# First loads in halves, fewer warm-up products and a reordered head in a gated dilated convolution

## The chip, the cores and the metric

The kernel runs on one core of a Trainium2 chip. The core has TensorE (PE) for matrix products, with its weight loads shown apart (PEld), VectorE (DVE), ScalarE (ACT), GpSimd (POOL) and SyncE (SP), which here only issues DMAs. Products go to PSUM, eight banks; everything else lies in SBUF. The metric is the time of one execution on the device in microseconds, the median of several runs; less is better.

## The reference

A causal convolution with three taps two tokens apart, a gate, and a projection. B = 2, T = 16000, D = 256, all in bfloat16:

```python
pad = 4
xp = jnp.pad(x, ((0, 0), (pad, 0), (0, 0)))
h = sum over i of 0, 1, 2:  xp[:, pad - 2*i : pad - 2*i + T, :] @ w[i]   # w: 3 x 256 x 512
z = jnp.tanh(h[..., :256]) * sigmoid(h[..., 256:])
return z @ w_o                                                           # w_o: 256 x 256
```

So a token needs itself, the token two back and the one four back. The notation of the sum is shortened; the reference adds the three products one after another.

## The kernel before, in words

Channels lie on partitions (256 channels are two halves, `ct` 0 and 1), tokens run along the free dimension, sorted by phase: token `4 r + j` or `8 r + j` is column `r` of phase `j`. Most of the work goes in "wide" groups of rows of eight tokens, whose tokens come by transposing DMAs (`load_wide`, L128). For them the three taps are not multiplied one by one: sums and differences of token phases (`wide_pairs` L221, `wide_p` L228, `wide_m` L232, `wide_d` L241, on DVE and in part on POOL) are multiplied by sums and differences of the taps' weights, in a scheme that needs fewer products than the three taps taken directly. The results are unscrambled by ACT (`keep_first` L286, `keep_second` L290), POOL (`other` L293) and DVE (`split_bank` L296, `rest` L300). Then ACT applies tanh and sigmoid (L340, L344), DVE multiplies the two (L349), PE projects (L374), and the result is copied out of PSUM and stored by SP.

A block is one group with 128 (plain) or, in the two narrow wide groups, 256 of the 512 output channels. `blocks` 0 to 3 are the plain group of the first 512 tokens, 4 and 5 the first wide group `G0`, 6 and 7 the second, `G1`, both 128 rows wide; later wide groups have 256 rows and four blocks each. Three small extra groups are multiplied directly beside them.

The schedule is written out by hand: every engine runs its instructions in the order in which the program issues them, and semaphores follow from the data and the buffers. The order of the head, which the change touches:

1. Loads (L141 to L145). SP: the first 512 tokens as 128 rows of four tokens (`xn`), then the taps `w_taps[TAPS[1]]`, that is tap 0. ACT: `TAPS[0]` (tap 2) and `TAPS[2]` (tap 1), then the table of functions. SP goes on with the transposing loads, one after another.
2. Seven warm-up products of 512 columns on constants (L149).
3. `turn` (L176 to L184) four times: for each half `h` of the phases and each half `ct` of the channels two PE transposes into a PSUM tile, and a copy to the plain group's tile `groups[0]["x"]`. For `h` 0 the PSUM tile is from the pool `ps_o` (two buffers), for `h` 1 from `ps_y` (three). The copies are ACT's for `ct` 0 and DVE's for `ct` 1.
4. The first tap of the four plain blocks (`direct`, L316): block 0 in two halves of the phases, blocks 1 to 3 whole. Then `weight_mm` (L170), six products that build combined weights in PSUM, then the second tap (tap 0) of the four blocks, and further on the third.
5. The combined weights: on DVE `plus2`/`minus2` (L440), `ws` (L444), `wmh` (L445) and `make_wu` (L455); on POOL `wph` (L446); on ACT `wd0`, `wm`, `wd2` (L447 to L449) and `make_wt` (L452). `make_wt` and `make_wu` of one `ct` read the same PSUM tile.
6. DVE's sums of `G0` and `G1`, and the first products of blocks 4 and 5 (`first`, L259).

From block 4 on a loop over the blocks (L553 to L632) issues for each: `second` and `keep_second`, `rest` of the block before, `third`, `split_bank`, the steps that the dictionaries `small`, `big` and `mid` hold for this block, and `late` in two parts. `late(V, 0)` adds to the two PSUM banks that `rest(V)` reads, and `late(V, 1)` adds to the same banks afterwards, so it waits for `rest(V)`. The list `mid[ND]` holds what DVE does behind block 4's `split_bank`.

Of the kernel before, what the change touches and what calls it, by code (L numbers as in the profile page):

```python
# [13 lines left out]
def kernel(  # L14
# [23 lines left out]
    nc = tc.nc  # L38
    bf16 = mybir.dt.bfloat16
    f32 = mybir.dt.float32  # L40
    B, T, D = x.shape
    K, _, D2 = w.shape
    P = 128
    assert K == 3 and D % P == 0 and D2 == 2 * D and T % 64 == 0
    CT = D // P
# [6 lines left out]
    TAPS = (2, 0, 1)  # L52
# [4 lines left out]
    for b in range(B):  # L57
        t, stop = (4 * 2 * P if b == 0 else 0), (T - 4 * RE if b == B - 1 else T)
        while t < stop:
            n = min(need, (stop - t) // 8)  # L60
# [23 lines left out]
    ps_y = ctx.enter_context(tc.tile_pool(name="ps_y", bufs=3, space=bass.MemoryType.PSUM))  # L84
    ps_o = ctx.enter_context(tc.tile_pool(name="ps_o", bufs=2, space=bass.MemoryType.PSUM))
    ctx.enter_context(tc.manual_schedule())

    def new_y():
        return ps_y.tile([P, 2, BANK], f32, name="y")
# [47 lines left out]
    w_taps = [consts.tile([P, CT, D2], bf16, name=f"w{k}_sb") for k in range(K)]  # L137
    wo_sb = consts.tile([P, NT, D], bf16)
    xn = osb_pool.tile([P, 4, D], bf16, name="osb")
    w_in = [w[k].rearrange("(ct c) d -> c ct d", c=P) for k in range(K)]  # L140
    nc.sync.dma_start(out=xn[:], in_=x[0, 0:4 * P, :].rearrange("(r j) c -> r j c", j=4))  # L141
    for k in (TAPS[0], TAPS[2]):
        nc.scalar.dma_start(out=w_taps[k][:], in_=w_in[k])
    nc.scalar.preload_act_table(ACT.Sigmoid)
    nc.sync.dma_start(out=w_taps[TAPS[1]][:], in_=w_in[TAPS[1]])  # L145
    for n in range(7):
        if n < 3:
            wps = new_y()
        nc.tensor.matmul(wps[:, 1, :], lhsT=warm[:, :P], rhs=warm, start=n < 3, stop=True, skip_group_check=True)  # L149
# [15 lines left out]
    def weight_mm():  # L165

        for ct in range(CT):
            y = W["y", ct] = ps_o.tile([P, D2], f32, name="wt_ps", tag="o_ps")
            for tap in (2, 0, 1):
                nc.tensor.matmul(  # L170
                    y[:], lhsT=twos[tap != 2][:], rhs=w_taps[tap][:, ct, :],
                    start=tap == 2, stop=tap == 1, skip_group_check=True,
                )


    def turn(h, ct):  # L176
        if h == 0:
            tp = ps_o.tile([P, 2, P], bf16, name="tp", tag="o_ps")[:]
        else:
            tp = ps_y.tile([P, 2, P], bf16, name="tq", tag="y")[:]  # L180
        for j in range(2):
            nc.tensor.transpose(out=tp[:, j, :], in_=xn[:, 2 * h + j, ct * P:(ct + 1) * P], identity=ident[:])  # L182
        copy = nc.vector.tensor_copy if ct % 2 else nc.scalar.copy
        copy(out=groups[0]["x"][:, 2 * h:2 * h + 2, ct, RH:RH + P], in_=tp)  # L184

    def views(G):
        xt, R = G["x"], G["R"]
        return xt[:, 0:2, :, RH - 1:RH - 1 + R], xt[:, 2:4, :, RH - 1:RH - 1 + R]

    def tap1_columns(G, ct):  # L190

        xt, R = G["x"], G["R"]
        lead = xt[:, 2:4, ct, RH - 1:RH - 1 + R]
        dims = [list(p) for p in lead.ap]
        return bass.AP(
            tensor=lead.tensor, offset=lead.offset,
            ap=[dims[0], [1 - 2 * CT * (RH + R), 2], [CT * (RH + R), 2], [1, R]],
        )

    def pair(G, i, back0, back1, col, rows):  # L200

        first = G["x"][:, 2 * i:2 * i + 2, :, col - back0:col - back0 + rows]
        dims = [list(p) for p in first.ap]
        return bass.AP(
            tensor=first.tensor, offset=first.offset,
            ap=[dims[0], [2 * CT * XW + back0 - back1, 2], [XW, 2 * CT], [1, rows]],
        )
# [3 lines left out]
    def sums(G, nm):  # L211
        if nm not in G:
            G[nm] = q_pool.tile(SUMS[nm], bf16, name=nm, bufs=3 if nm == "qd" else 2)
        return G[nm]

    def wide_pairs(G, h):

        for col, sl in G["cols"]:
            n = sl.stop - sl.start
            a, s = pair(G, 0, 0, 0, col, n), pair(G, 2, 0, 1, col, n)  # L220
            ins = nc.vector.tensor_tensor(  # L221
                out=sums(G, "q")[:, h, :, :, :, sl].rearrange("p h q ct r -> p h (q ct) r"),
                in0=s, in1=a, op=ALU.subtract if h else ALU.add)
        return ins

    def wide_p(G):
        q = G["q"][:, 0, :, :, :, :G["R"]]
        return nc.vector.tensor_tensor(out=sums(G, "qp")[..., :G["R"]], in0=q[:, 0], in1=q[:, 1], op=ALU.subtract)  # L228

    def wide_m(G, h):  # L230
        q = G["q"][:, h, :, :, :, :G["R"]]
        return nc.vector.tensor_tensor(out=sums(G, "qm")[:, h, ..., :G["R"]], in0=q[:, 0], in1=q[:, 1], op=ALU.add)  # L232
# [66 lines left out]
    def rest(B):  # L299
        nc.vector.tensor_tensor(out=B.sv[:], in0=B.sv[:], in1=B.y[:], op=ALU.subtract)  # L300

    def direct(B, taps, out, new=True, h0=None):

        xt, R = B.G["x"], B.R
        for tap in taps:
            if B.G is end:
                parts = [(None, xt[:, 4 - 2 * tap:8 - 2 * tap])]
            elif h0 is not None:
                parts = [(h0, views(B.G)[h0])]
            else:  # L310
                lo = RH if tap == 0 else RH - 1
                parts = [(None, xt[:, :, :, lo:lo + R])]
            for h, mv in parts:
                to = out if h is None else out[:, 2 * h * R:2 * (h + 1) * R]
                for ct in range(CT):
                    nc.tensor.matmul(  # L316
                        to, lhsT=w_taps[tap][:, ct, B.osl[0]],
                        rhs=tap1_columns(B.G, ct) if tap == 1 and B.G is not end else mv[:, :, ct, :],
                        start=new and tap == TAPS[0] and ct == 0 and not h, stop=tap == TAPS[-1] and ct == CT - 1,
                        skip_group_check=True,  # L320
                    )
# [96 lines left out]
    blocks = []  # L418
# [5 lines left out]
    ND = 4  # L424
    NB = len(blocks)

    def bank(B, i):
        return B.y[:, i % 2, :]

    for h in range(2):  # L430
        for ct in range(CT):
            turn(h, ct)
    for k in range(ND):
        blocks[k].y = new_y() if k % 2 == 0 else blocks[k - 1].y
    for h in range(2):
        direct(blocks[0], TAPS[:1], bank(blocks[0], 0), h0=h)
    for k in range(1, ND):
        direct(blocks[k], TAPS[:1], bank(blocks[k], k))
    for i, two in enumerate(twos):
        nc.vector.tensor_scalar_mul(two[:], ident[:], -2.0 if i else 2.0)  # L440
    weight_mm()
    for k in range(ND):
        direct(blocks[k], TAPS[1:2], bank(blocks[k], k))
    nc.vector.tensor_tensor(out=ws_sb[:], in0=w_taps[0][:], in1=w_taps[2][:], op=ALU.add)  # L444
    nc.vector.tensor_tensor(out=W["wmh"][:], in0=ws_sb[:], in1=w_taps[1][:], op=ALU.subtract)  # L445
# [5 lines left out]
    def make_wt(ct):  # L451
        return nc.scalar.copy(out=W["wt"][:, ct, :], in_=W["y", ct][:])  # L452

    def make_wu(ct):
        nc.vector.scalar_tensor_tensor(  # L455
            out=W["wu"][:, ct, :], in0=w_taps[1][:, ct, :], scalar=-4.0, in1=W["y", ct][:],
            op0=ALU.mult, op1=ALU.subtract)

    G0, G1 = groups[1:3]
    make_wu(0)  # L460
    make_wt(1)
    make_wu(1)
    make_wt(0)
    wide_pairs(G0, 0)
    wide_p(G0)
    for k in range(ND):
# [7 lines left out]
    wide_d(G0, 1, nc.vector)  # L474
    wide_d(G0, 0, nc.vector)
    wide_pairs(G1, 0)
    wide_p(G1)
    last = wide_m(G1, 0)

    def extra_block(i, taps):  # L480
        E = extras[i]
# [23 lines left out]
    small, big, mid = {}, {}, {}  # L505

    def do(steps, k):
        ins = None
        for step in steps.pop(k, []):
            ins = step() or ins  # L510
        return ins

    def gates_of(G, dts):
        if dts.stop == NT:
            ready.extend(pieces(G))
        return gate(G, dts)
# [4 lines left out]
        if B.oi % 2 == 1:  # L521
            big.setdefault(k + 1, []).append(lambda: gates_of(B.G, dts))

    mid[ND] = [lambda: wide_pairs(G1, 1)]
    mid[ND + 4] = [lambda: gates_of(extra, slice(0, 2))]
    mid[ND + 6] = [lambda: gates_of(end, slice(0, 2))]
    for G in wides[1:]:
# [25 lines left out]
    for k in range(ND, NB):  # L553
        B, V = blocks[k], (blocks[k - 1] if k > ND else None)
# [17 lines left out]
        last = do(small, k) or last  # L572
# [3 lines left out]
        def big_and_quarter(last):  # L576
            last = do(big, k) or last
            if B.G["n"] > 1 and B.oi == 0:
                quarter(B.G, 3, last)
            elif k in (ND + 2, ND + 3) or B.G["n"] > 1 and B.G["n"] + 1 < len(wides):  # L580
                for i in {ND + 2: (), ND + 3: (2,)}.get(k, (B.oi - 1,)):
                    quarter(wides[B.G["n"] + 1], i, last)
            return last

        if not big_late:
            last = big_and_quarter(last)
# [28 lines left out]
        last = do(mid, k) or last  # L615
        if big_late:
            last = big_and_quarter(last)
# [112 lines left out]
```

## Time and profile before

| | |
|---|---|
| median of 3 runs | 262.14 us (261.97 to 263.0) |
| profiled execution | 261.54 us, span 259.8 us |
| busy, share of the span | PE 254.9 us (98%), ACT 246.1 (95%), DVE 226.0 (87%), POOL 115.3 (44%) |
| instructions | PE 1491 products, 1491 weight loads, DVE 270, ACT 378, POOL 128 |
| DMA | 35.17 MB, 135 GB/s in the mean |

The span runs from the first to the last instruction of the program; the execution's time has 1.74 us around it. A line of the timeline reads: start in us, length, engine, line of the kernel, operation, names of output and inputs, shapes, count; in brackets the idle time of the engine before it and what ended it. A "q" behind an engine's name is its instruction queue, which also issues the DMAs. Matmuls overlap one another, so their lengths add up to more than the time that they take.

### The profile page before, as it was taken

What the parts mean: (1) busy time and instruction counts of PE and PEld (TensorE: products, weight loads), DVE (VectorE), ACT (ScalarE), POOL (GpSimd) and SP (SyncE); (2) the same over time, 40 slices, a digit from 0 to 9 for tenths busy, and PEclk for the clock granted to TensorE, in tenths of its full rate; (3) what the DMA queues carried; (4) which work ended last, traced back from release to release, by engine and by line L of the source; (5) the groups of instructions that cost most, each with busy time, mean ns of one, the idle gap of its engine ahead of it and who ended that gap; (6) DMA issues with size and microseconds to landing.
All of it is one profiled execution on the core that took longest, in us unless ns stands there. A gap on an engine that the chain in (4) does not pass through costs nothing.

```text
span 259.8 us, 4299 instructions
## 1 busy us (share of the span) xinstructions
PE 254.9 (98%) x1491; PEld 146.0 (56%) x1491; DVE 226.0 (87%) x270; ACT 246.1 (95%) x378; POOL 115.3 (44%) x128
## 2 busy tenths in 40 slices
PE   8999999999999999999999999999999999999993
PEld 4577765555555555555555555555555555555572
DVE  2889999988988988999988988988988988986673
ACT  5768889999999999999999999999999999999993
POOL 1432435445445445446445445445445445444240
PEclk9999999999999999999999999999999999999999
DMA  7999782471925628283481925728294221221226
GB/s 199 208 196 213 150 203 81 113 207 50 252 81 125 171 85 210 82 178 116 129 208 40 252 83 111 182 87 209 81 153 142 82 81 43 81 83 43 81 101 222
DMA packets 79685, 35.17 MB, mean 135 GB/s; under 512 B 69552, under 2 KB 72368, under 8 KB 79664
## 3 DMA queue, kind: packets, MB, share of 16 engines
q1 hardware_dynamic: 78560, 33.99, 52.1%
q10 hardware_dynamic: 1104, 0.92, 1.4%
q8 instruction: 11, 0.18, 0.3%
q14 instruction: 10, 0.08, 0.1%
HBM read 1.18 MB, written 16.38 MB: 68 GB/s over the span
## 4 chain that ended last, share of the span: by engine, by line
PE 97%; DVE 0%; ACT 0%; issue 0%; DVEq 0%; ACTq 0%
PE y L259 70%; PE o_ps L374 19%; PE y L316 2%; PE e_ps L316 2%; PE y L149 1%; PE y L374 1%; PE f_ps L316 1%; PE wt_ps L170 0%; DVE osb L674 0%; ACT osb L674 0%; PE tp L182 0%; PE tq L182 0%; DVEq L725 0%; ACT osb L672 0%; DVEq L672 0%
## 5 line engine op out<-in xcount | busy, mean ns | idle before, releaser
L293 POOL TENSOR_TENSOR sv<-sv,st 128x512 f32<-128x512 f32 x60 | 76.5, 1275 | 17.4 <-ACT sv L290 7.9
L241 POOL TENSOR_TENSOR qd<-xq 128x256 bf16<-128x256 bf16 (+2 forms) x58 | 33.7, 585 | 111.4 <-DVE zw L349 54.5
L300 DVE TENSOR_TENSOR sv<-sv,y 128x1024 f32<-128x1024 f32 x60 | 72.7, 1212 | 4.0 <-PE y L259 3.8
L259 PE MATMUL y<-qd,wd_sb 128*128 128x512 bf16 (+1 forms) x256 | 61.6, 366 | 0.0
L411 ACT CAST osb<-o_ps 128x512 bf16<-128x512 f32 x114 | 61.1, 591 | 0.0
L374 PE MATMUL o_ps<-wo_sb,zw 128*128 128x256 bf16 x450 | 58.9, 273 | 0.0
L296 DVE SCALAR_TENSOR_TENSOR y<-st,y 128x512 f32<-128x512 f32 x60 | 41.8, 696 | 19.6 <-PE y L259 11.1
L374 PEld LDWEIGHTS <-zw 128*128 128x128 bf16 x480 | 46.9, 98 | 17.4
L259 PE MATMUL y<-qp,wmh_sb 128*128 128x512 bf16 (+1 forms) x128 | 45.0, 366 | 0.0
L259 PEld LDWEIGHTS <-wd_sb 128*128 128x128 bf16 x256 | 25.0, 98 | 27.4 <-issue 0.5
L221 DVE TENSOR_TENSOR q<-xq 128x2048 bf16<-128x2048 bf16 (+3 forms) x34 | 37.9, 1119 | 0.9 <-DMA xq<-in_x_dram 0.8
L290 ACT ACTIVATE sv<-y 128x512 f32<-128x512 f32 x60 | 35.9, 598 | 0.9 <-PE y L259 0.7
L286 ACT ACTIVATE st<-y 128x512 f32<-128x512 f32 x60 | 36.3, 606 | 0.2 <-PE y L259 0.2
L259 PE MATMUL y<-q,wu_sb 128*128 128x512 bf16 (+1 forms) x128 | 35.7, 366 | 0.0
L259 PE MATMUL y<-qm,wph_sb 128*128 128x512 bf16 (+1 forms) x128 | 35.7, 366 | 0.0
L259 PE MATMUL y<-q,wt_sb 128*128 128x512 bf16 (+1 forms) x128 | 35.7, 366 | 0.0
L259 PE MATMUL y<-qm,wm_sb 128*128 128x512 bf16 (+1 forms) x128 | 35.7, 366 | 0.0
L349 DVE TENSOR_TENSOR zw<-thw,sgw 128x2048 bf16<-128x2048 bf16 x28 | 34.1, 1218 | 0.0
L340 ACT ACTIVATE sgw<-sv 128x1024 bf16<-128x1024 f32 x30 | 32.3, 1078 | 0.7 <-DVE sv L300 0.5
L340 ACT ACTIVATE thw<-sv 128x1024 bf16<-128x1024 f32 x30 | 32.3, 1078 | 0.3 <-DVE sv L300 0.3
L340 ACT ACTIVATE sgw<-y 128x1024 bf16<-128x1024 f32 x30 | 31.3, 1044 | 0.0
L340 ACT ACTIVATE thw<-y 128x1024 bf16<-128x1024 f32 x30 | 31.3, 1043 | 0.0
(68 smaller groups left out, 179.9 us busy)
## 6 DMA issues: line engine op xcount, KB each, us to landing
out_dram<-osb SPq DMA_DIRECT2D x54, 256.0 KB, 2.1
out_dram<-osb SPq DMA_DIRECT2D x10, 128.0 KB, 1.9
w_sb<-in_w_dram ACTq DMA_DIRECT2D x2, 256.0 KB, 4.2
out_dram<-osb SPq DMA_DIRECT2D x2, 160.0 KB, 2.0
xq<-in_x_dram SPq DMA_TRANSPOSE x17, 6.7
osb<-in_x_dram SPq DMA_DIRECT2D x1, 256.0 KB, 2.5
w_sb<-in_w_dram SPq DMA_DIRECT2D x1, 256.0 KB, 3.8
out_dram<-osb ACTq DMA_DIRECT2D x2, 128.0 KB, 2.1
```

What stands on the lines that cost most here:

```text
L221: ins = nc.vector.tensor_tensor(out=sums(G, "q")[:, h, :, :, :, sl].rearrange("p h q ct r -> p h (q ct) r"), in0=s, in1=a, op=ALU.subtract ...
L241: ins = after(eng.tensor_tensor(out=sums(G, "qd")[:, h, q, ct, sl], in0=a, in1=s, op=ALU.subtract), behind)
L259: nc.tensor.matmul(B.y[:, bank, i * n:(i + 1) * n], lhsT=wmat[:, ct, osl], rhs=mv[:, :, ct, :B.R], start=new and ct == 0 and i == 0, stop= ...
L286: nc.scalar.mul(B.st[:], B.y[:, 0, :], 4.0)
L290: nc.scalar.mul(B.sv[:, 0], B.y[:, 0, :], 2.0)
L293: after(nc.gpsimd.tensor_tensor(out=B.sv[:, 1], in0=B.sv[:, 0], in1=B.st[:], op=ALU.subtract), behind)
L296: nc.vector.scalar_tensor_tensor(out=B.y[:, 1, :], in0=B.st[:], scalar=-0.5, in1=B.y[:, 0, :], op0=ALU.mult, op1=ALU.add)
L300: nc.vector.tensor_tensor(out=B.sv[:], in0=B.sv[:], in1=B.y[:], op=ALU.subtract)
L340: nc.scalar.activation(out=dst[:, :, ph].rearrange("p b j c -> p j b c"), in_=at[:].rearrange("p j (b c) -> p j b c", b=hi - lo), func=fun ...
L349: return eng.tensor_tensor(out=z, in0=th, in1=sg, op=ALU.mult)
L374: nc.tensor.matmul(o_ps[q] if isinstance(o_ps, list) else o_ps[:, q, :], lhsT=z_columns(G, rb0, jp, q, dt), rhs=wo_sb[:, dt, :], start=(dt ...
L411: copy(out=G["osb"][:, 2 * h:2 * h + 2, :], in_=o_ps)
```

## The change

- The load of the first tokens becomes two loads by phases (`xn[:, 0:2]`, `xn[:, 2:4]`), both on SP, ahead of tap 0. The load of tap 2 becomes two loads by channels, both on ACT, ahead of tap 1.
- Five warm-up products instead of seven.
- `turn` takes all four PSUM tiles from `ps_o`. The copies are DVE's, but for `(h, ct) = (1, 0)`, which is ACT's.
- The first tap goes by quarters, that is phases half `h` and channels half `ct`, each for all four blocks: sixteen products of 256 columns, in the order (0, 0), (1, 0), (0, 1), (1, 1), with `turn(1, 1)` behind the first quarter and the other three `turn`s ahead of it.
- The second tap of blocks 0 and 1 goes ahead of `weight_mm`.
- `make_wu` and `make_wt` go in the order wu 0, wt 0, wu 1, wt 1 instead of wu 0, wt 1, wu 1, wt 0.
- `wide_m(G1, 0)` moves from ahead of the loop to the first place of `mid[ND]`. POOL's `other` of block 4, which was ordered behind it, is ordered behind `wide_p(G1)`.

```diff
-    nc.sync.dma_start(out=xn[:], in_=x[0, 0:4 * P, :].rearrange("(r j) c -> r j c", j=4))
-    for k in (TAPS[0], TAPS[2]):
-        nc.scalar.dma_start(out=w_taps[k][:], in_=w_in[k])
+    for h in range(2):
+        nc.sync.dma_start(
+            out=xn[:, 2 * h:2 * h + 2, :], in_=x[0, 0:4 * P, :].rearrange("(r j) c -> r j c", j=4)[:, 2 * h:2 * h + 2, :])
+    for ct in range(CT):
+        nc.scalar.dma_start(out=w_taps[TAPS[0]][:, ct, :], in_=w_in[TAPS[0]][:, ct, :])
+    nc.scalar.dma_start(out=w_taps[TAPS[2]][:], in_=w_in[TAPS[2]])
...
-    for n in range(7):
+    for n in range(5):
...
     def turn(h, ct):
-        if h == 0:
-            tp = ps_o.tile([P, 2, P], bf16, name="tp", tag="o_ps")[:]
-        else:
-            tp = ps_y.tile([P, 2, P], bf16, name="tq", tag="y")[:]
+        tp = ps_o.tile([P, 2, P], bf16, name="tp", tag="o_ps")[:]
...
-        copy = nc.vector.tensor_copy if ct % 2 else nc.scalar.copy
+        copy = nc.scalar.copy if (h, ct) == (1, 0) else nc.vector.tensor_copy
...
-    def direct(B, taps, out, new=True, h0=None):
+    def direct(B, taps, out, new=True, h0=None, cts=range(CT)):
...
-                for ct in range(CT):
+                for ct in cts:
...
-    for h in range(2):
-        for ct in range(CT):
-            turn(h, ct)
+    def first_tap(h, ct):
+        for k in range(ND):
+            direct(blocks[k], TAPS[:1], bank(blocks[k], k), h0=h, cts=(ct,))
+
+    for ct in range(CT):
+        turn(0, ct)
+    turn(1, 0)
     for k in range(ND):
         blocks[k].y = new_y() if k % 2 == 0 else blocks[k - 1].y
+    first_tap(0, 0)
+    turn(1, 1)
+    first_tap(1, 0)
     for h in range(2):
-        direct(blocks[0], TAPS[:1], bank(blocks[0], 0), h0=h)
-    for k in range(1, ND):
-        direct(blocks[k], TAPS[:1], bank(blocks[k], k))
+        first_tap(h, 1)
     for i, two in enumerate(twos):
         nc.vector.tensor_scalar_mul(two[:], ident[:], -2.0 if i else 2.0)
+    for k in range(2):
+        direct(blocks[k], TAPS[1:2], bank(blocks[k], k))
     weight_mm()
-    for k in range(ND):
+    for k in range(2, ND):
         direct(blocks[k], TAPS[1:2], bank(blocks[k], k))
...
-    make_wu(0)
-    make_wt(1)
-    make_wu(1)
-    make_wt(0)
+    for ct in range(CT):
+        make_wu(ct)
+        make_wt(ct)
...
-    wide_p(G1)
-    last = wide_m(G1, 0)
+    last = wide_p(G1)
...
-    mid[ND] = [lambda: wide_pairs(G1, 1)]
+    mid[ND] = [lambda: wide_m(G1, 0), lambda: wide_pairs(G1, 1)]
```

## The prediction

> **What bounds the kernel now.** I read the page first, then busy time by stretch, then the chain in order of time, then the timeline of the first 23 us by engine. The page and the chain of what ended last:
>
> ```profile
> span 259.8 us, 4299 instructions
> PE 97%; DVE 0%; ACT 0%; issue 0%; DVEq 0%; ACTq 0%
> ```
>
> The chain is TensorE (PE) almost alone. By stretches (busy us and count for PE, PEld, VectorE = DVE, ScalarE = ACT, GpSimd = POOL; granted clock; DMA share; GB/s):
>
> ```profile
> 13.50:22.70 9.20, 9.20 (x70) 6.66 (x69) 8.77 (x12) 6.77 (x12) 3.55 (x3) 1.00 1.29 210
> 45.00:240.00 195.00, 195.00 (x1103) 107.73 (x1101) 176.74 (x202) 195.00 (x301) 94.03 (x105) 1.00 0.48 126
> ```
>
> PE has no hole in either, so from 0.77 us on every microsecond taken out of PE's queue ends the kernel earlier, unless another engine then ends last. DVE is the candidate: 8.77 of 9.20 us in the stretch behind the head, against 177 of 195 later. The change touches only the head, so the head's chain comes next (start, length, what):
>
> ```profile
> 0.77 3.15 PE y L149 x7
> 3.92 0.43 PE tp L182 x4
> 4.77 1.97 PE y L316 x10
> 6.74 1.29 PE wt_ps L170 x6
> 8.04 3.47 PE y L316 x16
> ```
>
> and the same products by form in the head (count, busy us, mean ns of one):
>
> ```profile
> L149 PE MATMUL y<-const-bfloat16-1.0 128*128 128x512 bf16 x7 | 3.1, 625 | 0.8 <-PEq L714 0.8
> L316 PE MATMUL y<-xt,w_sb 128*128 128x512 bf16 x22 | 5.1, 380 | 0.0
> L182 PE MATMUL tp<-ident,osb 128*128 128x128 bf16 x4 | 0.6, 311 | 0.0
> ```
>
> The same 512 columns take 625 ns from start to end in the warm-up and 380 behind it, so PE runs at about half rate at first. Sixteen products at full rate took 3.47, 0.217 each; four transposes at low rate 0.43, 0.107 each. The change of rate lies between the transposes and L316's first products, near 4.7 us.
>
> **The change part by part.** What the head waits for now:
>
> ```profile
> 0.73 1.00 ACTq L143 DMA_DIRECT2D w_sb<-in_w_dram  x2
> 0.74 0.40 SPq L141 DMA_DIRECT2D osb<-in_x_dram  x1
> 1.20 0.41 SPq L145 DMA_DIRECT2D w_sb<-in_w_dram  x1
> 1.65 4.70 SPq L128 DMA_TRANSPOSE xq<-in_x_dram  x1
> 2.44 0.15 PEld L149 LDWEIGHTS <-const-bfloat16-1.0 128*128 128x128 bf16 x1 [0.28 <-issue]
> 2.86 0.15 PEld L149 LDWEIGHTS <-const-bfloat16-1.0 128*128 128x128 bf16 x1 [0.28 <-issue]
> 4.17 0.37 ACT L184 COPY xt<-tp 128x256 bf16<-128x256 bf16 x1 [1.12 <-PE tp L182]
> 4.38 0.29 DVE L184 COPY xt<-tp 128x256 bf16<-128x256 bf16 x1 [4.38 <-PE tp L182]
> ```
>
> ```profile
> osb<-in_x_dram SPq DMA_DIRECT2D x1, 256.0 KB, 2.5
> w_sb<-in_w_dram ACTq DMA_DIRECT2D x1, 256.0 KB, 3.4
> q1 hardware_dynamic: 109, 0.22, 70.8%
> ```
>
> (The second row is ACT's load of the first tap, the issue before 1.18 us. The last is all that the DMA engines carried from 1.70 to 2.72: the tokens alone, 0.22 MB.)
>
> *Two warm-up products fewer.* A warm-up product follows the last by 0.42 (2.44 to 2.86). Five of them leave PE free at 2.86 instead of 3.7: 0.85 us.
>
> *Tokens in halves.* The whole lands 2.5 after 0.74, at 3.24. At 0.22 MB in 1.02 us its 0.26 MB were through by 2.9 and half of them by 2.3; with the 0.3 from last data to landing, the first half lands at 2.6 at the earliest and 3.24 at the latest. I take 2.9, since nothing but the tokens was in flight then: PE hardly waits. The second half is issued 0.4 later on SP; even at 3.6 it is in time for what follows.
>
> *Transposes and copies.* Four transposes take 2.9 to 3.3. The second one ends at 2.9 + 0.11 + 0.31 = 3.3, DVE copies until 3.6. All four transposing tiles now share the two `o_ps` buffers, so `turn(1, 0)` waits for that copy: a new wait, PE idle from 3.3 to about 3.65. Queued behind it on PE is everything else. Then two transposes (0.21) to 3.86, four quarter products at half rate (4 x 0.21 = 0.85) to 4.7, where the rate changes; then at full rate two transposes (0.11) and twelve products of 256 columns (12 x 0.109 = 1.3) to 6.15. The columns are the same (16 x 256 against 4 x 256 + 6 x 512). The copies behind them (0.37 on ACT, 0.29 on DVE) lie beside products. Before, this point was where L170 began: 6.74 in the chain less its 0.16 of drain, 6.58. **PE leads by about 0.42.** Bounds: 0.2 with the first half at 3.24 (half of the added 0.35 lies at low rate), 0.5 with it at 2.6.
>
> *Weights.* The first tap's halves land by about 4.2 together, as now (0.73 + 3.4), and are read from 3.86 and from 5.2: nothing. The third tap's load moves 0.5 back on ACT's queue. The second tap and all transposing loads move 0.46 back on SP's. The next rows carry what follows:
>
> ```profile
> 6.25 1.06 ACT L448 ACTIVATE wm_sb<-w_sb 128x1024 bf16<-128x1024 bf16 x1 [0.20 <-DMA w_sb<-in_w_dram]
> 6.47 1.23 DVE L445 TENSOR_TENSOR wmh_sb<-sv,w_sb 128x1024 bf16<-128x1024 f32 x1
> 8.76 0.69 DVE L455 SCALAR_TENSOR_TENSOR wu_sb<-w_sb,wt_ps 128x512 bf16<-128x512 bf16 x1 [0.46 <-ACT wt_sb L452]
> 9.36 0.88 DVE L221 TENSOR_TENSOR q<-xq 128x1024 bf16<-128x1024 bf16 x1
> 10.27 0.42 DVE L228 TENSOR_TENSOR qp<-q 128x512 bf16<-128x512 bf16 x1
> 11.34 1.06 PE L259 MATMUL y<-qp,wmh_sb 128*128 128x256 bf16 x8
> ```
>
> The third tap landed at 6.25; at 6.75 it still precedes L445, which a third copy on DVE moves to about 6.87. The new order of `make_wu` and `make_wt` takes away DVE's 0.46 of idle, so L221 comes at 9.36 + 0.40 - 0.46 = 9.30, and `qp` ends near 10.65. PE needs it at 11.34 - 0.42 = 10.92. So the order is worth nothing by itself, but without it `qp` would end at 11.1 and take 0.2 of the lead. Putting two blocks' tap ahead of `weight_mm` moves PE's work, adds none, and gives the third tap 0.87 more time.
>
> *What is late next.* DVE behind the head, and PE's two products that wait for it:
>
> ```profile
> 13.53 0.70 DVE L221 TENSOR_TENSOR q<-xq 128x1024 bf16<-128x1024 bf16 x1 [0.75 <-DMA xq<-in_x_dram]
> 14.26 0.42 DVE L228 TENSOR_TENSOR qp<-q 128x512 bf16<-128x512 bf16 x1
> 14.60 0.42 DVE L232 TENSOR_TENSOR qm<-q 128x512 bf16<-128x512 bf16 x1
> 15.13 0.70 DVE L296 SCALAR_TENSOR_TENSOR y<-st,y 128x512 f32<-128x512 f32 x1
> 15.73 1.26 DVE L221 TENSOR_TENSOR q<-xq 128x1024 bf16<-128x1024 bf16 x1
> 17.07 1.22 DVE L300 TENSOR_TENSOR sv<-sv,y 128x1024 f32<-128x1024 f32 x1
> 18.35 0.27 PE L259 MATMUL y<-qd,wd_sb 128*128 128x256 bf16 x1
> 20.29 1.23 DVE L221 TENSOR_TENSOR q<-xq 128x2048 bf16<-128x2048 bf16 x1
> 21.44 1.21 DVE L300 TENSOR_TENSOR sv<-sv,y 128x1024 f32<-128x1024 f32 x1
> 22.71 0.27 PE L259 MATMUL y<-qd,wd_sb 128*128 128x256 bf16 x1
> xq<-in_x_dram SPq DMA_TRANSPOSE x1, 9.8
> ```
>
> `late(V, 1)` writes the banks that `rest` (L300) reads. L300 ends at 18.29 and 22.65; PE's products start 0.06 behind, both times. PE has no slack against DVE at these two places, and DVE started at 13.53 when the second wide load landed. With PE 0.42 earlier and that load unmoved: L296 no longer behind L232 but at 15.13 - 0.42 = 14.71; the moved `wide_m` at +0.60 = 15.31; L221 at +0.34 = 15.65; L300 at +1.26 = 16.91, its end 18.13, PE at 18.18 instead of 17.93. **The lead falls from 0.42 to 0.17.** At 20.29 DVE waits for the third wide load (the last row: issued at 10.27, landed 9.8 later, 20.07). L221 can start at 20.2 at the earliest, so PE at 22.62: the lead is 0.09. The moved `wide_m` costs nothing else; its reader, the next block's `second`, stands behind the products at 18.35.
>
> Do the loads move? SP issues 0.46 later, but the first transposing load occupied SP for 4.70, while the engines were still filled with tokens and weights. Same bytes ahead of it, so I take +0.1 for the smaller pieces; bounds 0 and +0.46.
>
> **The sum.** The profiled execution took 261.54 (span 259.8 and 1.74 around it): -0.42, +0.25 at 18.35, +0.08 at 22.71, +0.1 for the loads is 261.55. The median shown, 262.14, is 0.6 above it, the highest, 263.0, 1.5 above. I read this as PE's rate changing later in those executions; each microsecond at half rate costs 0.5. There PE trails DVE and the loads by 0.6 more, so the lead stays PE's own: 262.14 - 0.42 = 261.72, and with the +0.1 **261.8**. That is 0.13% under before; 0.5% (1.31 us) is about what a measurement of this kernel can tell from no change.
>
> [...]
>
> **The rivals.**
> 1. *The whole lead survives, and stalls go.* For: DVE loses 0.46 of idle and wide loads could come no later. Against: L300's two zero slacks. 261.54 - 0.42 in a profile-like execution, 261.1; with a median like before, 261.4 at best. To pass 0.5% (260.83) PE would have to gain 1.31, more than the 0.85 removed.
> 2. *The rate changes later.* For: PE now idles some 0.35 to 0.4 inside the warm-up stretch, where it had no hole. Now it took products from 0.77 to about 4.7, 3.9 us. If that count began again at 3.65, the rate would change at 7.55, 2.9 later, half of it lost: 1.44. 262.14 - 0.42 + 1.44 = 263.2, slower than before. It decides as soon as the change of rate moves by more than 0.84 (twice the lead). Against: the hole is a tenth of the stretch, and the present stretch holds eight transposes, 0.86 of it, and still ends. [...]
> 3. *SP's later issue moves every wide load.* At +0.46, L300 ends at 18.5 and the third load lands at 20.5: PE at 23.1 instead of 22.71. 261.54 + 0.4 = 261.95 in a profile-like execution, some 262.4 at the median. Against: 4.70 us of SP at the first of them.
> 4. *The pieces change nothing*, because the first half lands with the whole at 3.24 and the wait for the copy eats the rest: 262.1.
>
> **How the numbers follow.** Forecast 0.55, rival 1 0.10, rival 2 0.17, rival 3 0.10, rival 4 0.08. The range 261.2 to 263.3 leaves out the best of rival 1 and the worst of rival 2. Faster by over 0.5% needs a median with a far earlier change of rate besides: 0.04. Slower by over 0.5% (263.45) is the upper half of rival 2 and a sum of 2 and 3: 0.14. Same: 0.82. Without rivals of the other sign: 261.4 to 262.2.
>
> **What would show it.** The first transpose's weight load near 2.9, a hole on PE at 3.3 to 3.7 released by DVE's copy; mean 256-column products near 450 ns in the first quarter and 272 later; L170 starting near 7.0 with tap products ahead of it; L221 at about 13.6 again released by the DMA; PE's holes at 18.2 and 22.6 ahead of `y<-qd,wd_sb`, with L300 as the releaser; PE unchanged from 45 on. Wrong would be: 256-column products still slow after 5 us (rival 2); the first wide load landing 0.4 later (rival 3); PE at 22.3 without a hole (rival 1).

## The result and the profile after

The changed kernel takes 263.36 us (median of 15, 262.54 to 263.91) against 262.02 before (median of 15, 261.35 to 263.0): a ratio of 1.0049, 95% interval 1.0038 to 1.0060. It is slower, by just under the 0.5% named in the prediction, and 0.06 us above the end of the range. The profiled execution took 263.09 us, span 261.3, against 261.54 and 259.8: 1.55 us more.

The page of the changed kernel, its span and its chain by engine:

```profile
span 261.3 us, 4310 instructions
PE 96%; DMA 1%; DVE 0%; ACT 0%; issue 0%; DVEq 0%; ACTq 0%
```

The chain is still PE's, but a DMA has come into it: the tokens. The stretches that bound the kernel before, of the changed kernel (columns as in the prediction):

```profile
13.50:22.70 9.20, 9.20 (x69) 6.55 (x68) 7.87 (x15) 7.09 (x12) 2.54 (x2) 1.00 1.17 186
45.00:240.00 195.00, 195.00 (x1104) 107.75 (x1102) 177.47 (x202) 195.00 (x302) 94.05 (x105) 1.00 0.49 126
```

PE has no hole in them, as before; the 195 us from 45 on hold 1104 products against 1103. So the time came in the head. Its timeline, changed kernel (start, length, engine, line, operation, count, idle time before it and what ended that):

```profile
0.77 2.29 PE L153 MATMUL y<-const-bfloat16-1.0 128*128 128x512 bf16 x5 [0.77 <-PEq L720]
3.44 0.61 PE L183 MATMUL tp<-ident,osb 128*128 128x128 bf16 x4 [0.38 <-DMA osb<-in_x_dram]
4.21 0.37 PE L183 MATMUL tp<-ident,osb 128*128 128x128 bf16 x2 [0.17 <-DVE xt L185]
4.38 1.06 PE L317 MATMUL y<-xt,w_sb 128*128 128x256 bf16 x4
5.24 0.42 PE L183 MATMUL tp<-ident,osb 128*128 128x128 bf16 x2
6.96 1.06 ACT L455 ACTIVATE wd_sb<-w_sb 128x1024 bf16<-128x1024 bf16 x1 [1.97 <-DMA w_sb<-in_w_dram]
7.07 1.23 DVE L452 TENSOR_TENSOR sv<-w_sb 128x1024 f32<-128x1024 bf16 x1 [0.88 <-DMA w_sb<-in_w_dram]
8.84 0.38 PE L174 MATMUL wt_ps<-w_sb,plus 128*128 128x512 bf16 x1
12.14 0.42 DVE L229 TENSOR_TENSOR qp<-q 128x512 bf16<-128x512 bf16 x1
12.74 1.06 PE L260 MATMUL y<-qp,wmh_sb 128*128 128x256 bf16 x8
```

and the products up to 11.3 us by form (count, busy us, mean ns):

```profile
L317 PE MATMUL y<-xt,w_sb 128*128 128x256 bf16 x16 | 3.8, 413 | 0.0
L317 PE MATMUL y<-xt,w_sb 128*128 128x512 bf16 x10 | 2.5, 379 | 0.0
```

Two rows of the kernel before and one of the changed kernel, for the account below (in the last the first twelve products are quarters, the other four the second tap):

```profile
4.69 2.06 PE L316 MATMUL y<-xt,w_sb 128*128 128x256 bf16 x10
6.58 0.38 PE L170 MATMUL wt_ps<-w_sb,plus 128*128 128x512 bf16 x1
5.45 3.56 PE L317 MATMUL y<-xt,w_sb 128*128 128x256 bf16 x16
```

The sixteen quarter products last 413 ns in the mean, though twice as long a product lasts 379 a little later: all sixteen ran at half rate. From 5.45 to 7.80 they start 0.214 us apart, about as far as products of 512 columns at full rate (0.217). In the trace's record of the clock the rate doubles at 7.94 us, against 4.67 before. The account: the first product starts at 4.38 instead of 4.69, 0.31 earlier; from there to the end of the first tap PE takes until 7.98, 3.60 us, against 1.89 before (4.69 to 6.58): 1.71 more. Together 1.40, and PE's first product with `qp` comes at 12.74 instead of 11.34, 1.40 later. The same 1.40 stands at the end of the head's two narrow places (19.75 against 18.35, 24.11 against 22.71), and 1.39 in the last products (256.69 against 255.30). The rest of the 1.55 lies behind the last products.

The loads (KB each, us from issue to landing), changed kernel:

```profile
osb<-in_x_dram SPq DMA_DIRECT2D x2, 128.0 KB, 2.7
w_sb<-in_w_dram SPq DMA_DIRECT2D x1, 256.0 KB, 5.3
w_sb<-in_w_dram ACTq DMA_DIRECT2D x1, 256.0 KB, 5.7
```

The first half of the tokens landed at 3.39, no earlier than the whole before (3.28), and the second tap at 6.94 instead of 4.97. So there are two suspects: the clock, which the account shows, and the loads, which it may hide, since PE came for the second tap only at 7.98 and for `qp` (ended at 12.56) only at 12.74.

### The profile page after: what moved, and what is told of

It reads as the page before. It is cut to its first block, busy times and chain, and to the rows that moved or that the text cites. A ratio compares the mean times of both kernels' runs of the same rounds, so it can differ in the third digit from the quotient of the medians.

```text
span 261.3 us, 4310 instructions
## 1 busy us (share of the span) xinstructions
PE 255.8 (98%) x1495; PEld 146.9 (56%) x1495; DVE 226.0 (86%) x271; ACT 245.8 (94%) x377; POOL 115.1 (44%) x128
## 4 chain that ended last, share of the span: by engine, by line
PE 96%; DMA 1%; DVE 0%; ACT 0%; issue 0%; DVEq 0%; ACTq 0%
PE y L260 70%; PE o_ps L375 19%; PE y L317 3%; PE e_ps L317 2%; DMA osb<-in_x_dram 1%; PE y L375 1%; PE f_ps L317 1%; PE wt_ps L174 0%; PE tp L183 0%; DVE osb L680 0%; ACT osb L680 0%; DVEq L731 0%; DVE xt L185 0%; ACT osb L678 0%; DVEq L678 0%
## 5 line engine op out<-in xcount | busy, mean ns | idle before, releaser
L222 DVE TENSOR_TENSOR q<-xq 128x2048 bf16<-128x2048 bf16 (+3 forms) x34 | 37.6, 1112 | 0.1
```

The costliest lines, as they stand in the source:

```text
L222: ins = nc.vector.tensor_tensor(out=sums(G, "q")[:, h, :, :, :, sl].rearrange("p h q ct r -> p h (q ct) r"), in0=s, in1=a, op=ALU.subtract ...
```

## The experiments

Each kernel is timed against the kernel before, run beside it on the same chip; ratios are to that. The kernel before had a median of 261.61 us beside the first four kernels below; 261.98 beside those with transposes as warm-up, with one halving, and with the order alone; 261.86 beside those with fillers, with six products, with the quarters alone, and with own banks.

### Clock or loads: four kernels

Theory C says the late clock is the loss, theory L the late loads, theory B that each is enough.

*Seven warm-up products in the changed kernel.*

```diff
-    for n in range(5):
+    for n in range(7):
```

> The changed kernel with seven warm-up products again. Theory C (clock): with five, PE stands still or transposes for most of 2.9 to 4.4 us, its rate changes one step later (7.94 instead of 4.67 us in the two profiles), and that alone is the loss; the late weights (second tap landed at 6.96 instead of 4.97) are covered by PE's slow products. Then seven bring the rate change back to about 4.7 and the time to 261.7 to 262.2. Theory L (loads): the halved loads make the second tap land 2 us later, DVE's chain to qp ends at about 12.5 whatever PE does; the time stays at 263.0 to 263.5. Theory B (both, each enough by itself): fast products from about 4.7 on, then PE waits for the second tap or for qp; time near 263.

262.82 us (6 runs), ratio 1.0040 (1.0027 to 1.0052). PE's timeline:

```profile
3.71 0.51 PE L183 MATMUL tp<-ident,osb 128*128 128x128 bf16 x4
5.23 1.49 PE L317 MATMUL y<-xt,w_sb 128*128 128x256 bf16 x12
7.47 1.04 PE L317 MATMUL y<-xt,w_sb 128*128 128x512 bf16 x4 [0.75 <-DMA w_sb<-in_w_dram]
13.08 0.70 PE L260 MATMUL y<-qp,wmh_sb 128*128 128x256 bf16 x5 [0.68 <-DVE qp L229]
```

The rate doubles at 3.97 and the twelve products take 1.49 us. Then PE stands 0.75 us for the second tap (it landed at 7.42) and 0.68 for `qp`. Its first product with `qp` comes at 13.08, later than in the changed kernel (12.74), though the clock was in time. Theory C falls in its claim that the late weights are covered once the clock is in time; theory B has what it said.

*Five in the kernel before*, the one part alone.

```diff
-    for n in range(7):
+    for n in range(5):
```

> The kernel before with five warm-up products and nothing else changed: whole loads, tokens land at 3.24 us, so PE has a hole of about 0.4 from 2.9 to 3.3. Theory C and theory B: the rate changes at about 8 us, some 3.3 later than in the kernel before, less the 0.4 that the transposes come earlier: 263.0 to 263.6. Theory L: loads are untouched, so 261.7 to 262.1, no later rate change.

263.00 us (6 runs), ratio 1.0048 (1.0029 to 1.0066), as large a loss as the whole change. Products up to 9.8 us by form:

```profile
L316 PE MATMUL y<-xt,w_sb 128*128 128x512 bf16 x6 | 2.8, 630 | 0.0
L149 PE MATMUL y<-const-bfloat16-1.0 128*128 128x512 bf16 x5 | 2.3, 621 | 0.8 <-PEq L714 0.8
L182 PE MATMUL tp<-ident,osb 128*128 128x128 bf16 x4 | 0.6, 308 | 0.7 <-DMA osb<-in_x_dram 0.7
```

The first tap's products last 630 ns like the warm-up's 621; the rate doubles at 9.84. New are two products fewer and, in their place, PE's wait for the tokens, 0.7 as the profile counts it. Theory L falls as the only cause.

*Whole loads in the changed kernel, five products.*

```diff
-    for h in range(2):
-        nc.sync.dma_start(
-            out=xn[:, 2 * h:2 * h + 2, :], in_=x[0, 0:4 * P, :].rearrange("(r j) c -> r j c", j=4)[:, 2 * h:2 * h + 2, :])
-    for ct in range(CT):
-        nc.scalar.dma_start(out=w_taps[TAPS[0]][:, ct, :], in_=w_in[TAPS[0]][:, ct, :])
-    nc.scalar.dma_start(out=w_taps[TAPS[2]][:], in_=w_in[TAPS[2]])
+    nc.sync.dma_start(out=xn[:], in_=x[0, 0:4 * P, :].rearrange("(r j) c -> r j c", j=4))
+    for k in (TAPS[0], TAPS[2]):
+        nc.scalar.dma_start(out=w_taps[k][:], in_=w_in[k])
```

> The changed kernel with whole loads (tokens in one, first tap in one) and still five warm-up products. Theory C: the rate change stays late, 263.0 to 263.6; the second tap lands near 5 us again without use. Theory L: DVE's chain is early again, 261.6 to 262.1. Theory B: as theory C, 263.0 to 263.6, since the late clock is enough by itself.

263.76 us (6 runs), ratio 1.0070 (1.0053 to 1.0087), slower than any of the theories had it. The second tap lands at 5.12 again, the rate doubles at 8.64, the sixteen products last 418 ns:

```profile
L314 PE MATMUL y<-xt,w_sb 128*128 128x256 bf16 x16 | 3.8, 418 | 0.0
w_sb<-in_w_dram SPq DMA_DIRECT2D x1, 256.0 KB, 3.9
```

The loads in time save nothing while the clock is late.

*Whole loads and seven products.* The two edits together:

> The changed kernel with whole loads and seven warm-up products: what is left is quarters, the transposing tiles in one pool, the copies and the order of DVE's and ACT's weight work. Theory C and theory B: 261.7 to 262.2, like the kernel before; theory L the same. If it is near 263.3, the cause is in the quarters or the order and all three theories fall. In theory B it is the one of this call's four that is fast.

262.56 us (5 runs), ratio 1.0032 (1.0019 to 1.0044); the rate doubles at 4.80, the sixteen products last 275 ns. It is the fastest of the four, but not the 262.2 that all theories allowed. PE has lost little to the clock or the first loads (its `qp` product starts at 11.49, against 11.34 before); it loses 0.78 between 15.9 and 19.3, behind DVE:

```profile
14.63 0.69 DVE L219 TENSOR_TENSOR q<-xq 128x1024 bf16<-128x1024 bf16 x1 [1.13 <-DMA xq<-in_x_dram]
18.01 1.20 DVE L298 TENSOR_TENSOR sv<-sv,y 128x1024 f32<-128x1024 f32 x1
19.27 0.93 PE L257 MATMUL y<-qd,wd_sb 128*128 128x256 bf16 x7 [0.26 <-DVE sv L298]
```

The second wide load landed at 14.61 here, 1.1 later than in the profile before, and `rest` (L298) and the product behind it pay. That is the narrow place of the prediction, met from the other side.

The four ratios side by side:

| changed kernel with | five products | seven products |
|---|---|---|
| halved loads | 1.0049 (the change) | 1.0040 |
| whole loads | 1.0070 | 1.0032 |

With whole loads the intervals of five and seven lie apart: the late clock costs 0.4%. With halved loads they overlap: the profile shows the gained clock being lost again to the waits for the loads. Between halved and whole loads at seven products the intervals overlap too, so for the loads' share of the time there are the waits in the profile and the kernel with one halving alone (1.0034, below), but no clear difference here. The kernel before with both halvings and nothing else was not run.

### Holes or the number of products

*Fillers in the changed kernel.* Its five products and halved loads stay; eight transposes of a constant are put into PE's two holes.

```diff
+    fill = ps_y.tile([P, 2, P], bf16, name="tw", tag="y")[:]
+
+    def filler(n):
+        for _ in range(n):
+            nc.tensor.transpose(out=fill[:, 0, :], in_=warm[:, :P], identity=ident[:])
+
+    filler(5)
     for ct in range(CT):
         turn(0, ct)
+    filler(3)
     turn(1, 0)
```

> The changed kernel with its five warm-up products and halved loads, and with eight transposes of a constant in PE's two holes: five ahead of the first real transposes, three behind the fourth. If the holes are what delays the rate change, it comes at 4 to 5 us although there are no more products; PE then waits for the second tap and for qp as with seven products: 262.5 to 262.9, some 0.5 under the changed kernel. If the number of products counts, the rate change stays at 7.5 to 8.5 and the time at 263.2 to 263.6.

The rate doubles at 5.11 instead of 7.94, with no product more. So the holes are what kept it, as far as one profile of each shows. PE's timeline:

```profile
2.86 0.74 PE L439 MATMUL tw<-ident,const-bfloat16-1.0 128*128 128x128 bf16 x5
3.98 0.52 PE L439 MATMUL tw<-ident,const-bfloat16-1.0 128*128 128x128 bf16 x3
5.36 1.49 PE L317 MATMUL y<-xt,w_sb 128*128 128x256 bf16 x12
7.99 1.04 PE L317 MATMUL y<-xt,w_sb 128*128 128x512 bf16 x4 [1.13 <-DMA w_sb<-in_w_dram]
13.60 0.60 PE L260 MATMUL y<-qp,wmh_sb 128*128 128x256 bf16 x4 [0.68 <-DVE qp L229]
```

The time missed what was expected: 263.19 us (6 runs, 262.50 to 264.43), ratio 1.0060 (1.0038 to 1.0083). The second tap landed later still, at 7.94, and PE gave the gained clock back waiting for it (1.13) and for `qp` (0.68). Part of the miss is no work of the kernel: in three of the six runs 2.0, 2.25 and 3.03 us of the time lie outside the span, where the runs of the kernel before beside them have 1.74 to 1.86. The median span is 261.15 against 260.0 before, 1.15 more; that the fillers win or lose anything against the changed kernel is not shown. Theory B holds so far as the profiles show it: the clock and the late taps each hold PE up by more than a microsecond, and they do not add.

*Transposes in place of warm-up products, kernel before.*

```diff
-    for n in range(7):
-        if n < 3:
-            wps = new_y()
-        nc.tensor.matmul(wps[:, 1, :], lhsT=warm[:, :P], rhs=warm, start=n < 3, stop=True, skip_group_check=True)
+    for n in range(3):
+        wps = new_y()
+        nc.tensor.matmul(wps[:, 1, :], lhsT=warm[:, :P], rhs=warm, start=True, stop=True, skip_group_check=True)
...
+    wtp = ps_y.tile([P, 2, P], bf16, name="tw", tag="y")[:]
+    for n in range(16):
+        nc.tensor.transpose(out=wtp[:, 0, :], in_=warm[:, :P], identity=ident[:])
```

> The kernel before with sixteen transposes of a constant in place of four of the seven warm-up products: PE is as busy without a hole, for the same 1.71 us, but transposes fill most of the stretch ahead of the rate change. If what the clock counts is PE being busy with anything, the rate changes at 4 to 5 us and the time is 261.4 to 262.0. If transposes do not count as products do, the stretch fails as it does with five products: rate change at 7.5 to 8.5 us and 262.8 to 263.6.

262.21 us (12 runs), ratio 1.0015 (0.9999 to 1.0032): the same within the measurement, or up to 0.3% slower, and between the two ranges that were expected. In the profile the rate doubles at 5.39:

```profile
0.77 1.44 PE L148 MATMUL y<-const-bfloat16-1.0 128*128 128x512 bf16 x3 [0.77 <-PEq L716]
2.01 1.91 PE L153 MATMUL tw<-ident,const-bfloat16-1.0 128*128 128x128 bf16 x16
4.68 2.24 PE L318 MATMUL y<-xt,w_sb 128*128 128x256 bf16 x10
```

From 2.01 to 4.57 PE did nothing but transposes, and the rate doubled at 5.39, not at the 7.5 to 8.5 that was expected if they do not count.

*Six warm-up products, kernel before*, the version that could have beaten both.

```diff
-    for n in range(7):
+    for n in range(6):
```

> The kernel before with six warm-up products, nothing else changed. [...] If any hole spoils the stretch, 262.8 or more.

261.76 us (12 runs), ratio 0.9997 (0.9984 to 1.0011): no difference. PE waited for the tokens until 3.63 in the profile (they landed at 3.58), and the rate doubled at 5.37. No version that beats the kernel before was found.

### The halves one at a time, kernel before

*Tokens in halves.*

```diff
-    nc.sync.dma_start(out=xn[:], in_=x[0, 0:4 * P, :].rearrange("(r j) c -> r j c", j=4))
+    for h in range(2):
+        nc.sync.dma_start(
+            out=xn[:, 2 * h:2 * h + 2, :], in_=x[0, 0:4 * P, :].rearrange("(r j) c -> r j c", j=4)[:, 2 * h:2 * h + 2, :])
```

> The kernel before with only the tokens loaded in two halves. If it is the tokens' halves that hold up the second tap's load behind them on SP: it lands near 7 instead of 5 us, DVE's chain to qp ends near 12.4, PE waits there about 0.9, time 262.4 to 262.9. If it is the tap's halves: second tap near 5.4 us (issued 0.45 later), time 261.5 to 262.1.

262.19 us (10 runs), ratio 1.0010 (0.9995 to 1.0026): no clear difference.

*First tap in halves.*

```diff
-    for k in (TAPS[0], TAPS[2]):
-        nc.scalar.dma_start(out=w_taps[k][:], in_=w_in[k])
+    for ct in range(CT):
+        nc.scalar.dma_start(out=w_taps[TAPS[0]][:, ct, :], in_=w_in[TAPS[0]][:, ct, :])
+    nc.scalar.dma_start(out=w_taps[TAPS[2]][:], in_=w_in[TAPS[2]])
```

> The kernel before with only the first tap loaded in two halves by channels. The other way round: if the tap's halves hold up the other taps, the second or third tap lands near 7 us and the time is 262.4 to 262.9; if it is the tokens' halves, the second tap lands near 5 us, the third near 6.7, time 261.5 to 262.1. If both e6 and e7 are like before, only the two together fill the queues.

262.61 us (10 runs), ratio 1.0034 (1.0014 to 1.0053). The times of the last landing in the profiles:

| kernel | tokens | second tap | third tap |
|---|---|---|---|
| before | 3.28 | 4.97 | 6.22 |
| tokens in halves | 3.48 and 4.58 | 6.14 | 5.33 |
| first tap in halves | 4.30 | 6.05 | 6.73 |
| both (changed kernel) | 3.39 and 4.03 | 6.94 | 7.35 |

Either halving brings the second tap about one microsecond later, both about two. Each row is one profile; in the nine profiles of kernels with whole loads the second tap landed between 4.97 and 5.60 and the tokens between 3.28 and 3.77, so the effect of one halving may be half as large. With both halvings the other two profiles have the second tap at 7.42 and 7.94. Neither expectation had it so: it was to be the one or the other. In the kernel with the first tap in halves the tokens, which are not touched, landed late too, at 4.30. That the halving did this is not shown: from 1.8 to 2.4 us, ahead of any data of the tap, 0.02 MB of tokens moved there, against 0.11 before. PE in that kernel:

```profile
4.34 0.61 PE L183 MATMUL tp<-ident,osb 128*128 128x128 bf16 x4 [0.43 <-DMA osb<-in_x_dram]
5.29 2.61 PE L317 MATMUL y<-xt,w_sb 128*128 128x256 bf16 x10
```

The transposes wait until 4.34 even with seven warm-up products. The rate doubles at 6.73; that it does so for that wait, one profile does not show.

### Order and quarters

*The order alone, kernel before.*

```diff
+    for k in range(2):
+        direct(blocks[k], TAPS[1:2], bank(blocks[k], k))
     weight_mm()
-    for k in range(ND):
+    for k in range(2, ND):
...
-    make_wu(0)
-    make_wt(1)
-    make_wu(1)
-    make_wt(0)
+    for ct in range(CT):
+        make_wu(ct)
+        make_wt(ct)
...
-    wide_p(G1)
-    last = wide_m(G1, 0)
+    last = wide_p(G1)
...
-    mid[ND] = [lambda: wide_pairs(G1, 1)]
+    mid[ND] = [lambda: wide_m(G1, 0), lambda: wide_pairs(G1, 1)]
```

> The kernel before with only the order changed: the second tap of blocks 0 and 1 ahead of the doubled weights, wu and wt in turn, the second group's first sum behind block 4's split. Loads, warm-up, transposes and first products as before. Theory B (clock and halved loads are the two causes, the order is neutral): 261.4 to 262.0, the same as before within 0.2%. Rival O (the order holds something up, since the changed kernel with whole loads and seven warm-up products was still 0.32% slower): 262.3 to 262.7, with PE's holes of some 0.7 between 15 and 20 us as there, although the second wide load lands by 13.6.

262.08 us (12 runs), ratio 1.0004 (0.9991 to 1.0017): neutral. The profiled execution shows the narrow place again, because its second wide load landed at 14.08: PE's product behind `rest` came at 18.74, after 0.26 of idle. The median is that of before all the same.

*The quarters alone* (seven products, whole loads, order of before; `turn`, the copies, `first_tap` and the sixteen products as changed).

```diff
-        if h == 0:
-            tp = ps_o.tile([P, 2, P], bf16, name="tp", tag="o_ps")[:]
-        else:
-            tp = ps_y.tile([P, 2, P], bf16, name="tq", tag="y")[:]
+        tp = ps_o.tile([P, 2, P], bf16, name="tp", tag="o_ps")[:]
...
-        copy = nc.vector.tensor_copy if ct % 2 else nc.scalar.copy
+        copy = nc.scalar.copy if (h, ct) == (1, 0) else nc.vector.tensor_copy
...
-    for h in range(2):
-        for ct in range(CT):
-            turn(h, ct)
+    for ct in range(CT):
+        turn(0, ct)
+    turn(1, 0)
...
+    first_tap(0, 0)
+    turn(1, 1)
+    first_tap(1, 0)
     for h in range(2):
-        direct(blocks[0], TAPS[:1], bank(blocks[0], 0), h0=h)
-    for k in range(1, ND):
-        direct(blocks[k], TAPS[:1], bank(blocks[k], k))
+        first_tap(h, 1)
```

> The kernel before with only the head's quarters: the four transposing tiles from one pool, the copies moved to VectorE but one, sixteen products of 256 columns; whole loads, seven warm-up products, the order of before. If the quarters are what made the changed kernel with whole loads and seven products 0.32% slower than before: 262.3 to 262.7, PE waiting some 0.4 for the copy ahead of the third transposing. If they are neutral: 261.6 to 262.1, and that 0.32% belongs to quarters and order together.

262.19 us (12 runs), ratio 1.0018 (1.0007 to 1.0028): between the two expectations, a small loss.

*Quarters and order, with the second pair of transposing tiles in their own banks* (the changed kernel with whole loads and seven products, and `turn` thus):

```diff
-        tp = ps_o.tile([P, 2, P], bf16, name="tp", tag="o_ps")[:]
+        if h == 0:
+            tp = ps_o.tile([P, 2, P], bf16, name="tp", tag="o_ps")[:]
+        else:
+            tp = ps_y.tile([P, 2, P], bf16, name="tq", tag="y")[:]
```

> The changed kernel with whole loads, seven warm-up products and the transposing tiles in two pools as before, so that no transpose waits for a copy. If that new wait is what costs: PE has no hole between the transposes and the time is 0.2 to 0.4 under that of the changed kernel with whole loads and seven products (262.56): 262.1 to 262.4. If not, the same 262.5 and PE's holes of 0.5 to 0.8 between 15 and 20 us, behind a late second wide load.

262.19 us (12 runs), ratio 1.0023 (1.0010 to 1.0035), against 1.0032 (1.0019 to 1.0044) with one pool: the intervals overlap, so no gain from the banks is shown, though the 262.19 lies in the range expected for one: the kernel before was 0.25 slower beside this kernel than beside the other. What stays open is which part of the quarters costs the 0.2%. The second wide load's landing, 13.34 to 14.85 over the profiles of kernels with whole loads, moves PE's narrow place by more than that.

## Why the prediction was wrong

Two steps under the forecast, 261.8, did not hold: the moment of the clock's change, which set the measured time, and the landing of the loads, which stood behind it. Rival 2, with 263.2, is what happened. By the prediction's steps:

- **"four quarter products at half rate (4 x 0.21 = 0.85) to 4.7, where the rate changes".** This step failed. It took the moment of the kernel before for given, though the change puts holes ahead of it. The rate changed at 7.94, and the stretch with the sixteen products took 1.71 more than before. Rival 2 had the cause (a hole ahead of the change of rate), its sign (quarter products still slow after 5 us) and nearly the price: 1.44 less the lead of 0.42, where 1.71 less 0.31 was measured. Its count that begins again behind a hole is not what the runs show: the kernel with six products has a hole up to 3.63 and the full rate from 5.37 on. Its chance of 0.17 was too low, held down by "the hole is a tenth of the stretch". There were two holes, 2.86 to 3.44 and 3.84 to 4.21 (a product counted as the 0.427 us from one warm-up product's start to the next, a transpose as 0.107), together 0.95 us: about a quarter of the 3.9 us that the prediction counts, from 0.77 to 4.7. The median, 263.36, came 0.16 above rival 2's 263.2, in "the worst of rival 2" that the range left out.
- **"I take 2.9" for the first half of the tokens**, bounds 2.6 to 3.24. It landed at 3.39, outside the bounds. The bound from above took for granted that half the bytes land no later than the whole did; with the tokens alone in halves the first landed at 3.48, no sooner either. This made the first hole.
- **The new wait for the copy**, PE idle for about 0.35: it came, 3.84 to 4.21, released by DVE's copy as the timeline says. The prediction gave it a price of its own, but put the other hole, the wait for the tokens, at next to nothing and so did not add the two.
- **Weights and wide loads, "+0.1 for the smaller pieces".** The first wide load came 1.0 later (9.64 against 8.67), ten times that. The second tap, put 0.46 back, came 2.0 later, and the third, put 0.5 back, 1.1 (7.35 against 6.22). The late clock covered it; with the clock in time PE stood 1.43 for it in the profile (0.75 and 0.68), though the times do not set that apart from what the quarters cost (1.0040 and 1.0032).
- **The order "is worth nothing by itself"**: right, 1.0004 (0.9991 to 1.0017).
- **The narrow places.** PE has no slack against `rest` there: right. In the changed kernel the product comes 0.06 behind `rest` again (18.47 + 1.22 = 19.69, product at 19.75). **That the third wide load holds L221 at 20.29** was a misreading: in the changed kernel that load landed at 20.89, L222 started at 21.69, and the same 0.12 of idle stands before it. So the load was not what it waited for.
- **The spread between executions** was laid to the clock alone. For the changed kernel an estimate bears that out in the main. In its profile the full rate is on record from 7.94 us on and lasts 252.59, to 260.52, and the run's granted clock (0.998) is below 1 only for the half rate behind that. If the full rate lasted as long in the other runs, their spans and granted clocks put the doubling near 6.8 in the four shortest (spans of 260.8 to 261.0, clock 0.997) and at 9.0 or later in the four with a granted clock of 1.000 (261.9 to 262.1): about 1.1 us of span for some two us of delay or more. The estimate hangs on that length, which was 256.00 in the profile of before. The second wide load's landing moves as well (13.34 to 14.85 over the profiles of kernels with whole loads), so the clock is not all of it.

## What to carry to other kernels

Before warm-up work on PE is cut, add up PE's holes ahead of the change of rate, new waits included: here two products fewer, 0.85 us of PE, went with 0.95 us of holes, a change of rate 3.27 later and 1.71 more for the first tap. Do not count on the halves of a load to land sooner than the whole: the first half of the tokens landed at 3.39 and 3.48 here, the whole between 3.28 and 3.77. The profile's landing times of everything behind and beside a divided load have to be read, not only its own. Where two causes hold up the same engine at the same time, undoing one shows little, so undo each, both and neither before either is called the cause.

## What the runs showed of the hardware

The moment at which the rate doubles, from the trace's record of the clock, and PE's idle time ahead of it, from 0.77 us on, as the timeline counts it (to a product's end, so that the two holes of the changed kernel are 0.38 and 0.17 here):

| kernel | PE idle ahead of it, us | rate doubles at, us |
|---|---|---|
| changed, seven products | 0 | 3.97 |
| before | 0 | 4.67 |
| changed, whole loads, seven products | 0.17 | 4.80 |
| changed, filled | 0 | 5.11 |
| before, six products | 0.14 | 5.37 |
| before, transposes as warm-up | 0 | 5.39 |
| before, first tap in halves | 0.43 | 6.73 |
| changed | 0.55 | 7.94 |
| before, five products | 0.70 | 9.84 |

In the changed kernel with whole loads and five products the rate doubles at 8.64. PE stands 0.2 us idle there behind DVE's copy, besides its wait for the tokens, which landed 2.8 us after their issue. In these profiles the late moments, 6.73 to 9.84, go with the longer holes, the early ones, 3.97 to 5.39, with none or with one of 0.14 or 0.17. The kernel with the tokens alone in halves lies between: 0.39 us idle, and its first ten products of the tap took 2.21 us, against 2.29 in the kernel with six products and 3.57 in the one with five. Each row is one profile. By what rule PE's holes move the moment, the runs do not show, nor how far it moves between executions of one kernel: in the four profiles without idle time it lies from 3.97 to 5.39.

No run sets transposes apart from products in this. The kernel with transposes as warm-up has sixteen of them in place of four products, and its rate doubled at 5.39, against 9.84 with five products. In the filled kernel eight more transposes, and no product more, went with 5.11 instead of 7.94.

That the 512 KB behind 512 KB of loads cut into four pieces land later, the second tap at 6.94 against 4.97 and the third at 7.35 against 6.22, was not expected either. Why is open: from 3.6 to 4.2 us the trace has 0.06 MB of loads moved in the changed kernel against 0.22 before (0.05 and 0.10 in the other two kernels with both halvings, 0.23 in either kernel with one), and what held them back it does not show.
